# Local attention and a top-2 expert layer on one core: row tiles, a constant copy and weight splits on other turns, list products a turn behind GpSimd

## The chip, the cores and the metric

One core of a Trainium2 chip runs the whole program. The metric is the device time of one execution in microseconds; a kernel's number is the median of its runs. The engines are named as the profile names them: PE is TensorE (PEld its weight loads), DVE is VectorE, ACT is ScalarE, POOL is GpSimd, and SP is SyncE, which issues most DMAs.

## The reference

The work is an attention within chunks of 64 positions, followed by a layer of eight experts of which each token uses two.

```python
scores = scale * np.matmul(q_c, k_c.transpose(0, 1, 2, 4, 3))      # chunks of 64
attn = np.exp(scores - scores.max(-1)); attn /= attn.sum(-1) + 1e-9
x = (attn @ v_c) as (4608 tokens, 512)
noisy_logits = x @ w_gate + np.log1p(np.exp(x @ w_noise)) * noise   # (4608, 8)
top2 and their softmax weights, per token
for e in range(8):                                                  # w1 512x1024, w2 1024x512
    out[mask] += weight * (np.maximum(x[mask] @ w1[e], 0.0) @ w2[e])
```

All data are float32. The large products are made of three products of rounded halves (`three`, L305): each operand is split into a high part `h` and a rest `l`, and the product of the two rests is left out.

## The kernel before, in words

**Turns.** The tokens are 36 tiles of 128. `attend(it)` (L677) is one turn of a software pipeline over the tiles: in turn `it` PE computes the scores of tile `it` (L410), the value products of tile `it - 2` (L437), the transposed probabilities of tile `it - 1` (L426) and the transposed rows of tile `it - 3` (L457). Every fourth turn adds a gate product (L464), the next turn its sum (L476). DVE takes the maximum (`mx`, L414) and the difference (`pr`, L419) of the new tile, and the reciprocal and scaling (`rc`, `xs`) of tile `it - 2`. ACT does the exponential and the copies out of PSUM. SP loads q, k and v four turns ahead and stores each finished tile to `xbuf` in DRAM.

**Routing.** The tiles form five groups of 8, 8, 4, 8 and 8 tiles (numbered 0 to 4 here, `LAST` is 4). When the gate values of a group are there, a Python generator `route(g)` (L481) issues the group's routing in small pieces, and `step_route(n)` takes n pieces. So the number of pieces per turn sets where each routing instruction stands in the queues of all engines. A turn takes 10 pieces up to turn 34 and 15 after that; in the layers of the first two blocks each hook takes 2. The pieces of a group, in order: ACT's four functions (L494 to L497), seven empty pieces, five gate steps on DVE (`gu`, `gsp`), the eight-wide maxima and their indices (`gm`, `gmi`), the one-hot rows (`goh`) and their sum `gohb` (L527), seven empty pieces ahead of the rank products on PE (L535, L537), the ranks back on DVE (`gr`, L546), and then `gpf` (L582), the place of every token in the lists.

**List rows and list products.** After that the group has one row for each tile (L595 to L614). A row is a pair of one-hot matrices `gohp` (one half by POOL, L598, the other by two ACT functions, L599 and L600) and a matrix `grhs` (from `geq` on DVE, L602; the product on POOL, L606, for the last group on DVE). `place` (L588) multiplies the two on PE into bank 7 of PSUM (L590). A row is multiplied after two more have been built; three buffers of each operand hold them. At a group's end DVE adds the bank to `acc` (L622, L624), and after groups 1, 3 and 4 the lists of one block of expert 0 are finished and its rows gathered.

**Blocks.** Each expert's rows come in three blocks. `x_tile(i, k)` (L279) turns one tile of 128 gathered rows of block i (for the first three blocks four PE transposes, L288) and splits it (`xh` by ACT, `xl` by DVE). `layer1` (L307) and `layer2` (L346) then run the products; layer 1 of block 0 starts right behind the last turns, whose rests (turns 37 to 40) are put between its products by `hook_tail`. Block 0's three tiles are turned at the end of turns 33, 34 and 35 into PSUM banks 6, 6 and 5. Block 1's three tiles are turned within layer 2 of block 0, after the seventh of eight product triples of each row tile (hook `hook2_r`, L777). In layer 2 of block 1, `pieces()` (L215) copies the identity into `spread` (`xv`) and multiplies it with the lists (L222, L224) to make the row numbers for all later gathers.

**Splits.** Expert 0's first weights come in eight half loads (turns 11 to 18) and are split by `w_split` (L130) in turns 18, 19, 21, 22, 24, 25, 27 and 28: high part on ACT (L137), rest on POOL (L138).

All engines have their own queue in program order, so an instruction that waits holds everything behind it on its engine.

Of the kernel before, what the change touches and what calls it, by code (L numbers as in the profile page):

```python
# [8 lines left out]
FT = mybir.dt.float32  # L9
# [10 lines left out]
P = 128  # L20
NTOK = 4608
NT = NTOK // P
# [38 lines left out]
def kernel(ctx, tc, qT, kT, vh, wgn, noise, w1, w2, out, caps=CAPS):  # L61
    nc = tc.nc
# [10 lines left out]
    ident = consts.tile([P, P], FT, name="ident")  # L73
# [27 lines left out]
    for c in sorted(set(caps[1:])):  # L101
        n = caps.index(c, 1)
# [14 lines left out]
    place = {}  # L117
# [38 lines left out]

    NPE = nb
    AHEAD = [(1, 7), (2, 2), (2, 4), (2, 7)]
    LATE = [(1, 0), (1, 4), (2, 0), (2, 4)]
    groups = [(0, 8), (8, 8), (16, 4), (20, 8), (28, 8)]  # L160
    LAST = len(groups) - 1
# [6 lines left out]
    NL = NJ * NE  # L168
# [44 lines left out]
    xv = []  # L213

    def pieces():  # L215

        spread = xv[0].tile([P, 4, 4, 32], FT, name="xv")
        nc.vector.tensor_copy(spread, ident.rearrange("p (t c) -> p t c", t=4)[:, :, None, :].to_broadcast([P, 4, 4, 32]))
        tf = lfl
        for t in range(4):  # L220
            p = PS[:, 7, t * NJ * NE:(t + 1) * NJ * NE]
            nc.tensor.matmul(p, spread[:, t].rearrange("p a c -> p (a c)"), tf.rearrange("p j e -> p (j e)"),  # L222
                             start=True, stop=True)
            nc.tensor.matmul(PS[:, 7, 4 * NJ * NE + t * NE:4 * NJ * NE + (t + 1) * NE],  # L224
                             spread[:, t].rearrange("p a c -> p (a c)"), lwt[:, NJ - 1, :], start=True, stop=True)
        nc.vector.tensor_copy(wrep.rearrange("p t e -> p (t e)"), PS[:, 7, 4 * NJ * NE:4 * (NJ + 1) * NE])
        nc.vector.tensor_scalar(piece.rearrange("p t j e -> p (t j e)"), PS[:, 7, 0:4 * NJ * NE],
                                4.0, part, op0=OP.mult, op1=OP.add)
# [248 lines left out]
        nc.scalar.activation(Z[q][:, 4 * g - t0:4 * g - t0 + 4].rearrange("p g a e -> p (g a e)"), PS[:, 6, 0:64], AF.Copy)  # L477

    IDLE = 7

    def route(g):  # L481

# [102 lines left out]
        lp = PS[:, 7, 0:2 * NL]  # L585
        built = []

        def place(r, ohp, rhs):  # L588
            for k in range(2):
                nc.tensor.matmul(lp, ohp[:, k], rhs[:, k].rearrange("p c n -> p (c n)"),  # L590
                                 start=(r == 0 and k == 0), stop=(r == G - 1 and k == 1))

        B = nc.gpsimd if g < LAST else V
        n2 = [P, 2, NL]
        for r in range(G):  # L595
            t = t0 + r
            ohp = gate.tile([P, 2, P], FT, name="gohp", bufs=3)
            nc.gpsimd.tensor_scalar(ohp[:, 0], row_p, pf[:, 0, 0, r:r + 1], None, op0=OP.is_equal)  # L598
            nc.scalar.activation(ohp[:, 1], row_p, AF.Abs, scale=-1.0, bias=pf[:, 0, 1, r:r + 1])  # L599
            nc.scalar.activation(ohp[:, 1], ohp[:, 1], AF.Relu, scale=-1.0, bias=1.0)  # L600
            eq = gate.tile(n2, FT, name="geq", bufs=3)
            V.tensor_tensor(eq, row_je.rearrange("p j e -> p (j e)")[:, None, :].to_broadcast(n2),  # L602
                            pf[:, 1, :, r:r + 1].to_broadcast(n2), OP.is_equal)
            yield
            rhs = gate.tile([P, 2, 2, NL], FT, name="grhs", bufs=3)
            B.tensor_tensor(rhs, eq[:, :, None, :].to_broadcast([P, 2, 2, NL]),  # L606
                            vals[:, :, t, :, None].to_broadcast([P, 2, 2, NL]), OP.mult)
            yield
            yield
            built.append((r, ohp, rhs))  # L610
            if len(built) > 2:
                yield
                place(*built.pop(0))
            yield  # L614
        while built:
            for _ in range(3):
                yield
            place(*built.pop(0))
        yield
# [11 lines left out]
        if g == LAST:  # L631
            for c in range(2):
                for js in (slice(0, NJ // 2), slice(NJ // 2, NJ)):
                    n = [P, js.stop - js.start, NE, NE]
                    by = gate.tile([P, 2, 2, NL], FT, name="grhs", bufs=3).rearrange("p a b n -> p (a b n)")
                    by = by[:, 0:n[1] * NE * NE].rearrange("p (j r e) -> p j r e", r=NE, e=NE)
                    V.tensor_tensor(by, a4[:, c, js][:, :, None, :].to_broadcast(n),
                                    perm[:, None].to_broadcast(n), OP.mult)
                    V.tensor_reduce(accp[:, c, js], by, AX.X, OP.add)
                    yield  # L640
            finish_lists(lid, lwt, lfl, accp)
# [2 lines left out]

    def step_route(n):
        for _ in range(n):
            while routing:
                try:
                    next(routing[0])
                    break  # L650
                except StopIteration:
                    routing.pop(0)
# [22 lines left out]
        nc.sync.dma_start(staged[0, which, c][:, h * 512:h * 512 + 512], src)  # L675

    def attend(it):  # L677
        STEPS = 2 if it < 35 else 3
        if it < NT:
            scores(it)  # L680
        if it + 4 < NT:
            load_q(it + 4)
            load_k(it + 4)
        if 0 <= it - 2 < NT:
            pv(it - 2)
        if it + 4 < NT:
            load_v(it + 4)
        if 0 <= it - 2 < NT:
            norm_a(it - 2)
        if 0 <= it - 1 < NT:  # L690
            p_trans(it - 1)
        if 0 <= it - 3 < NT:
            x_trans(it - 3)
        if it - 5 >= 0 and (it - 5) % 4 == 3:
            gate_sum((it - 5) // 4)
            if grp_of[it - 5] != grp_of.get(it - 4):
                routing.append(route(grp_of[it - 5]))
        if it - 4 >= 0 and (it - 4) % 4 == 3:
            gate_mm((it - 4) // 4)
        if it < NT:  # L700
            soft_sub(it, soft_max(it))
            soft_exp(it)
        if 0 <= it - 2 < NT:
            norm_b(it - 2)
            norm_c(it - 2)
            if 0 <= it - (NT - 3) < 3:
                x_tile(0, it - (NT - 3), at=(6, 6, 5)[it - (NT - 3)])
            step_route(5 * STEPS)
        if it in (18, 19, 21, 22, 24, 25, 27, 28):
            w_split(0, 1, *wq.pop(0), eng=nc.gpsimd)  # L710
        if 11 <= it < 19:
            half_load(1, it - 11)
        if NT - 8 <= it < NT:
            half_load(2, it - NT + 8)
        if it == 8:
            nc.sync.dma_start(xbuf[0:P, :], zero)
        if NT - 3 <= it < NT:
            zero_out(2)
# [30 lines left out]
    for i in range(NBL + 1):  # L749
# [27 lines left out]
        def hook2_r(k, f):  # L777
            hook2_f(k, f)
            step_route(2)
            if i == 0 and f == 6 and k < len(nxt):  # L780
                x_tile(1, k)
            if i == 1 and (k, f) in LATE:
                x_tile(2, LATE.index((k, f)))
            if i == 1 and (k, f) == (1, 5):
# [23 lines left out]
        elif i == 1:  # L808
# [3 lines left out]
            xy = pb.enter_context(tc.tile_pool(name="xy", bufs=2))  # L812
            HF[0] = pb.enter_context(tc.tile_pool(name="hf", bufs=1)).tile([P, NF, max(c % P for c in caps[1:])], FT, name="hf")
            xv.append(pb.enter_context(tc.tile_pool(name="xv", bufs=1)))
            layer2(1, hook2_r)
        elif i != 2 and i != 3:
            layer2(i - 1, hook2_f)
# [135 lines left out]
```

## Time and profile before

| what | value |
| --- | --- |
| median of 3 runs | 997.32 us (996.1 to 998.82) |
| the profiled execution, as timed | 996.2 us |
| its span, first to last instruction | 994.4 us |
| mean granted TensorE clock | 0.99 |
| PE busy | 955.1 us (96%) |
| DVE, ACT, POOL busy | 459.3, 307.9, 485.4 us |
| HBM traffic over the span | 121 GB/s |

The profile comes from one execution. Its times count from the first instruction. A row of a timeline has the start, the duration, the engine, the line, the operation and its tiles (out<-in); a bracket at its end has the time the engine was idle just before it, and who ended that. Rows of the chain have start, length, engine, tile and line; there and in the timelines a float32 matmul is recorded as two, so that "x4" of L590 is one list row with its two products. "issue" is a wait for which the profile shows nothing.

### The profile page before, as it was taken

Reading aid. Unit: us, or ns where it says so; the run is one execution under the profiler, and the core shown is the slowest. Engines: PE = TensorE matmul, PEld = TensorE weight load, DVE = VectorE, ACT = ScalarE, POOL = GpSimd, SP = SyncE. Lnnn points to the kernel's source line nnn. Section 1 sums busy time; section 2 is a strip of 40 time slices with the busy share of each in tenths; the row PEclk is TensorE's granted clock in tenths of the full one; section 3 lists DMA queues with packets and bytes.
Section 4 is the critical chain, followed back from the end, with each engine's and each line's share of the span. In section 5 each row is a group of like instructions: output and inputs, shape, how many; then the busy total and the mean of one; then the engine's idle time right before and its main releaser. Section 6 shows DMA issues by size and latency. Waiting matters only on the chain.

```text
span 994.4 us, 18553 instructions
## 1 busy us (share of the span) xinstructions
PE 955.1 (96%) x7353; PEld 855.4 (86%) x7353; DVE 459.3 (46%) x1001; ACT 307.9 (31%) x689; POOL 485.4 (49%) x619
## 2 busy tenths in 40 slices
PE   6898989999999999999999999999999999999994
PEld 5677769888799998998899899989998999899984
DVE  6678876543445442534253434343444344434311
ACT  4667764312232221322131223122322231223100
POOL 1043534426677776177617772677167616601111
PEclk9989999999999999999999999999999999999998
DMA  9998968332513452245214522552245223511212
GB/s 336 377 340 271 323 228 310 63 102 54 146 46 81 111 151 50 44 122 150 51 33 128 148 51 36 135 140 58 68 96 140 58 70 94 136 20 22 32 25 41
DMA packets 60362, 121.54 MB, mean 122 GB/s; under 512 B 9280, under 2 KB 10176, under 8 KB 60272
## 3 DMA queue, kind: packets, MB, share of 16 engines
q1 hardware_dynamic: 40112, 81.64, 23.2%
q0 software_dynamic: 20160, 38.69, 20.8%
q8 instruction: 58, 0.95, 0.4%
q14 instruction: 32, 0.26, 0.1%
HBM read 81.56 MB, written 38.73 MB: 121 GB/s over the span
## 4 chain that ended last, share of the span: by engine, by line
PE 84%; DVE 2%; ACT 1%; issue 0%; POOL 0%; DVEq 0%; ACTq 0%; POOLq 0%
PE PS L305 80%; PE PS L590 1%; PE PS L334 1%; PE PS L288 0%; DVE xl L296 0%; ACT xh L295 0%; PE PS L464 0%; DVE o L343 0%; POOL grhs L606 0%; DVE xs L449 0%; PE PS L222 0%; ACT xt L458 0%; PE PS L437 0%; ACT gohp L599 0%; DVE gmi L518 0%
## 5 line engine op out<-in xcount | busy, mean ns | idle before, releaser
L260 POOL DMA_INDIRECT xg<-xbuf,piece x257 | 265.9, 1035 | 72.6 <-issue 66.3
L305 PE MATMUL PS<-xh,w1h 128*128 128x384 f32 (+2 forms) x768 | 262.9, 342 | 1.9 <-ACT xh L295 1.1
L305 PE MATMUL PS<-xl,w1h 128*128 128x384 f32 (+2 forms) x768 | 260.5, 339 | 0.3 <-DVE xl L296 0.3
L305 PE MATMUL PS<-xh,w1l 128*128 128x384 f32 (+2 forms) x768 | 260.6, 339 | 0.0
L272 POOL DMA_INDIRECT out<-o,lid x73 | 116.9, 1601 | 246.5 <-DVE o L343 234.4
L305 PE MATMUL PS<-w2h,hh 128*128 128x512 f32 x584 | 229.5, 393 | 0.0
L305 PE MATMUL PS<-w2h,hl 128*128 128x512 f32 x584 | 228.4, 391 | 0.0
L305 PE MATMUL PS<-w2l,hh 128*128 128x512 f32 x584 | 228.3, 391 | 0.0
L323 ACT ACTIVATE hh<-PS 128x384 fp32r<-128x384 f32 (+1 forms) x192 | 93.9, 490 | 362.3 <-PE PS L305 362.3
L324 DVE SCALAR_TENSOR_TENSOR hl<-PS,hh 128x384 fp32r<-128x384 f32 (+1 forms) x192 | 107.0, 558 | 181.1 <-ACT hh L323 181.1
L343 DVE TENSOR_SCALAR o<-PS,lwt 128x512 f32<-128x512 f32 x73 | 54.7, 749 | 235.4 <-PE PS L305 235.4
L305 PEld LDWEIGHTS PS<-xh,w1h 128*128 128x128 f32 x768 | 144.3, 188 | 5.4 <-ACT xh L295 1.5
L305 PEld LDWEIGHTS PS<-xl,w1h 128*128 128x128 f32 x768 | 144.3, 188 | 2.3 <-DVE xl L296 0.5
L305 PEld LDWEIGHTS PS<-xh,w1l 128*128 128x128 f32 x768 | 144.2, 188 | 0.9
L305 PEld LDWEIGHTS PS<-w2h,hl 128*128 128x128 f32 x584 | 109.5, 188 | 23.6
L305 PEld LDWEIGHTS PS<-w2h,hh 128*128 128x128 f32 x584 | 109.7, 188 | 23.2 <-issue 0.8
L305 PEld LDWEIGHTS PS<-w2l,hh 128*128 128x128 f32 x584 | 109.7, 188 | 22.4
L295 ACT ACTIVATE xh<-y 128x512 fp32r<-128x512 f32 x67 | 41.2, 615 | 104.8 <-DVE y L292 104.8
L598 POOL TENSOR_SCALAR gohp<-row_p,gpf 128x128 f32<-128x128 f32 x36 | 25.1, 707 | 95.8 <-DVE gpf L582 71.6
L296 DVE TENSOR_TENSOR xl<-y,xh 128x512 fp32r<-128x512 f32 x67 | 45.0, 672 | 48.0 <-ACT xh L295 48.0
L292 DVE STREAM_TRANSPOSE y<-xg 128x512 f32<-128x512 f32 x67 | 45.6, 680 | 3.2 <-DMA xg<-xbuf,piece 3.2
L138 DVE TENSOR_TENSOR w2l<-st,w2h 128x512 fp32r<-128x512 f32 x64 | 44.4, 693 | 0.0
(139 smaller groups left out, 783.7 us busy)
## 6 DMA issues: line engine op xcount, KB each, us to landing
st<-in_w SPq DMA_DIRECT2D x56, 512.0 KB, 5.0
out<-zero SPq DMA_DIRECT2D x37, 256.0 KB, 4.0
vb<-in_vh SPq DMA_DIRECT2D x36, 260.0 KB, 4.9
qp<-in_qT SPq DMA_DIRECT2D x36, 256.0 KB, 4.5
kb<-in_kT SPq DMA_DIRECT2D x36, 256.0 KB, 5.3
xbuf<-xs SPq DMA_DIRECT2D x36, 256.0 KB, 4.4
xg<-xbuf,piece POOLq DMA_INDIRECT x257, 2.7
st<-in_w SPq DMA_DIRECT2D x16, 256.0 KB, 5.7
```

The lines of the kernel that those rows point to most:

```text
L138: (eng or nc.vector).tensor_sub(lo[:, s], st[:, s], hi[:, s].bitcast(FT))
L260: nc.gpsimd.indirect_dma_start(out=XG[e, j][:, t * P:(t + 1) * P], out_offset=None, in_=xpieces, in_offset=bass.IndirectOffsetOnAxis(ap=pi ...
L272: s = nc.gpsimd.indirect_dma_start(out=to, out_offset=bass.IndirectOffsetOnAxis(ap=rows, axis=0), in_=o, in_offset=None, compute_op=OP.add)
L292: nc.vector.transpose(y[:, 0:4 * r], x[:, 0:4 * r])
L295: nc.scalar.activation(oh, src, AF.Copy)
L296: nc.vector.tensor_sub(ol, src, oh.bitcast(FT))
L305: nc.tensor.matmul(p, a, b, start=first and n == 0, stop=last and n == 2)
L323: nc.scalar.activation(hh[:, 0:m], p, AF.Relu)
L324: nc.vector.scalar_tensor_tensor(hl[:, 0:m], p, 0.0, hh[:, 0:m].bitcast(FT), op0=OP.max, op1=OP.subtract)
L334: nc.tensor.matmul(p[32 * q:32 * q + 32, 0:P], HF[0][:, f, 32 * t:32 * t + 32], w[:, q * P:(q + 1) * P], start=(f == 0), stop=(f == NF - 1))
L343: nc.vector.tensor_scalar(o[0:r], p[0:r], weights_of(i, j)[0:r], None, op0=OP.mult)
L598: nc.gpsimd.tensor_scalar(ohp[:, 0], row_p, pf[:, 0, 0, r:r + 1], None, op0=OP.is_equal)
```

## The change

It does five things; none changes what is computed.

1. A turn takes 11 pieces of routing instead of 10 up to turn 34, 15 after that as before.
2. A list row is multiplied when it is `LAG` pieces old (9 up to turn 35, 6 after that) or when more than two wait, at the start of the next row; the rows' operands get four buffers each.
3. Block 0's third tile is turned at the start of turn 36 into bank 0, not at the end of turn 35 into bank 5. Block 1's three tiles are turned after triple 6 of row tile 0 and triples 2 and 6 of row tile 1 (counted from 0).
4. The splits stand in turns 21 to 25 and 30 to 32, the half loads in turns 13 to 20.
5. `spread` is copied ahead of layer 2 of block 1, not within `pieces()`.

```diff
+    SECOND = [(0, 6), (1, 2), (1, 6)]
...
     def pieces():
-        spread = xv[0].tile([P, 4, 4, 32], FT, name="xv")
-        nc.vector.tensor_copy(spread, ident.rearrange(...).to_broadcast([P, 4, 4, 32]))
+        spread = xv[1]
...
+    clock, LAG = [0], [9]
...
         for r in range(G):
+            while built and (clock[0] - built[0][3] >= LAG[0] or len(built) > 2):
+                place(*built.pop(0))
             t = t0 + r
-            ohp = gate.tile([P, 2, P], FT, name="gohp", bufs=3)
+            ohp = gate.tile([P, 2, P], FT, name="gohp", bufs=4)
...
             yield
             yield
-            built.append((r, ohp, rhs))
-            if len(built) > 2:
-                yield
-                place(*built.pop(0))
+            yield
+            built.append((r, ohp, rhs, clock[0]))
             yield
         while built:
-            for _ in range(3):
+            while clock[0] - built[0][3] < LAG[0]:
                 yield
             place(*built.pop(0))
...
     def step_route(n):
         for _ in range(n):
+            clock[0] += 1
...
     def attend(it):
-        STEPS = 2 if it < 35 else 3
+        LAG[0] = 9 if it < NT else 6
         if it < NT:
             scores(it)
+        if it == NT:
+            x_tile(0, 2, at=0)
...
-            if 0 <= it - (NT - 3) < 3:
-                x_tile(0, it - (NT - 3), at=(6, 6, 5)[it - (NT - 3)])
-            step_route(5 * STEPS)
-        if it in (18, 19, 21, 22, 24, 25, 27, 28):
+            if 0 <= it - (NT - 3) < 2:
+                x_tile(0, it - (NT - 3), at=6)
+            step_route(11 if it < 35 else 15)
+        if it in (21, 22, 23, 24, 25, 30, 31, 32):
             w_split(0, 1, *wq.pop(0), eng=nc.gpsimd)
-        if 11 <= it < 19:
-            half_load(1, it - 11)
+        if 13 <= it < 21:
+            half_load(1, it - 13)
...
-            if i == 0 and f == 6 and k < len(nxt):
-                x_tile(1, k)
+            if i == 0 and (k, f) in SECOND:
+                x_tile(1, SECOND.index((k, f)))
...
             xv.append(pb.enter_context(tc.tile_pool(name="xv", bufs=1)))
+            xv.append(xv[0].tile([P, 4, 4, 32], FT, name="xv"))
+            nc.vector.tensor_copy(xv[1], ident.rearrange(...).to_broadcast([P, 4, 4, 32]))
             layer2(1, hook2_r)
```

Three places show how the queues change. The first is PE's queue in turns 14 and 15, before: scores (L410), value products, the two transposes, and in turn 15 the gate product and the rank products of group 0.

```order
L410 MATMUL PS<-kb,qp 64x64 x16
L437 MATMUL PS<-vb,pts 64x65 x16
L426 MATMUL PS<-ident,pr 128x128 x4
L457 MATMUL PS<-ident,xs 128x128 x4
L410 MATMUL PS<-kb,qp 64x64 x16
L437 MATMUL PS<-vb,pts 64x65 x16
L426 MATMUL PS<-ident,pr 128x128 x4
L457 MATMUL PS<-ident,xs 128x128 x4
L464 MATMUL PS<-xt,wg 32x512 x4
L535 LDWEIGHTS before
L535 MATMUL PS<-gohb,before 128x72
```

The same queue of the changed kernel, from the scores of turn 14 on:

```order
L410 MATMUL PS<-kb,qp 64x64 x16
L437 MATMUL PS<-vb,pts 64x65 x16
L426 MATMUL PS<-ident,pr 128x128 x4
L457 MATMUL PS<-ident,xs 128x128 x4
L536 LDWEIGHTS before
L536 MATMUL PS<-gohb,before 128x72
L538 LDWEIGHTS ones
L538 MATMUL PS<-gohb,ones 128x64
```

The rank products now stand ahead of the scores of turn 15, in the turn in which DVE makes `gohb`. The same holds for group 2 in turn 30 and group 3 in turn 36.

The second place is PE's queue behind the last tile's value products (L437), where layer 1 of block 0 (L305) has begun. Before, group 3's first list product comes 33 matmuls of layer 1 behind them; these are the rows just ahead of it:

```order
L305 MATMUL PS<-xh_136,w1l_2170 128x384
L476 MATMUL PS<-sel,ls 128x16 x4
L305 MATMUL PS<-xh_136,w1h_1426 128x384
L305 MATMUL PS<-xl_137,w1h_1426 128x384
L305 MATMUL PS<-xh_136,w1l_1427 128x384
L590 MATMUL PS<-grhs,gohp 128x160 x2
```

In the changed kernel the whole stretch from the value products to that first list product (now L591) is this:

```order
L437 MATMUL PS<-vb,pts 64x65 x16
L457 MATMUL PS<-ident,xs 128x128 x4
L305 MATMUL PS<-xh_136,w1h_2014 128x384
L305 MATMUL PS<-xl_137,w1h_2014 128x384
L305 MATMUL PS<-xh_136,w1l_2015 128x384
L591 MATMUL PS<-grhs,gohp 128x160 x2
L305 MATMUL PS<-xh_136,w1h_2507 128x384
```

Only one transpose and three matmuls of layer 1 are left between them.

The third place is DVE's queue at the end of layer 2 of block 0: `gpf` and the list rows (`geq`, `grhs`) of group 4, the third row tile of block 1 (`xl`), and the weighing of a finished row tile (`o`). Before:

```order
L576 TENSOR_TENSOR vals<-gex,vals 128x8
L580 TENSOR_SCALAR gpj<-lii 128x16
L581 TENSOR_TENSOR gpj<-lii,gpj 128x16
L582 CAST gpf<-gpj 128x32
L602 TENSOR_TENSOR geq<-row_je,gpf 128x160
L606 TENSOR_TENSOR grhs<-geq,vals 128x320
L602 TENSOR_TENSOR geq<-row_je,gpf 128x160
L296 TENSOR_TENSOR xl_3251<-PS,xh_3250 128x4x128
L606 TENSOR_TENSOR grhs<-geq,vals 128x320
```

And in the changed kernel:

```order
L577 TENSOR_TENSOR vals<-gex,vals 128x8
L296 TENSOR_TENSOR xl_3268<-PS,xh_3267 128x4x128
L581 TENSOR_SCALAR gpj<-lii 128x16
L582 TENSOR_TENSOR gpj<-lii,gpj 128x16
L583 CAST gpf<-gpj 128x32
L605 TENSOR_TENSOR geq<-row_je,gpf 128x160
L343 TENSOR_SCALAR o<-PS,lwt_126 128x512
L609 TENSOR_TENSOR grhs<-geq,vals 128x320
```

The row tile's `xl` has moved from behind two list rows to ahead of the first.

More of the change, by code (lines that the diff above doesn't have):

```diff
@@ L215, in pieces @@
     def pieces():
-        spread = xv[0].tile([P, 4, 4, 32], FT, name="xv")
-        nc.vector.tensor_copy(spread, ident.rearrange("p (t c) -> p t c", t=4)[:, :, None, :].to_broadcast([P, 4, 4, 32]))
+        spread = xv[1]
         tf = lfl
@@ L586, in route, with place @@
         built = []
-        def place(r, ohp, rhs):
+        def place(r, ohp, rhs, at):
             for k in range(2):
@@ L604, in route @@
             yield
-            rhs = gate.tile([P, 2, 2, NL], FT, name="grhs", bufs=3)
+            rhs = gate.tile([P, 2, 2, NL], FT, name="grhs", bufs=4)
             B.tensor_tensor(rhs, eq[:, :, None, :].to_broadcast([P, 2, 2, NL]),
@@ L634, in route @@
                     n = [P, js.stop - js.start, NE, NE]
-                    by = gate.tile([P, 2, 2, NL], FT, name="grhs", bufs=3).rearrange("p a b n -> p (a b n)")
+                    by = gate.tile([P, 2, 2, NL], FT, name="grhs", bufs=4).rearrange("p a b n -> p (a b n)")
                     by = by[:, 0:n[1] * NE * NE].rearrange("p (j r e) -> p j r e", r=NE, e=NE)
@@ L814 @@
             xv.append(pb.enter_context(tc.tile_pool(name="xv", bufs=1)))
+            xv.append(xv[0].tile([P, 4, 4, 32], FT, name="xv"))
+            nc.vector.tensor_copy(xv[1], ident.rearrange("p (t c) -> p t c", t=4)[:, :, None, :].to_broadcast([P, 4, 4, 32]))
             layer2(1, hook2_r)
```

## The prediction

> **What bounds the kernel now.** I read the busy times by stage first, then the vector engine's waits in the first of those stages, then the timeline at each place the diff touches. Columns of the first view: stretch, its length, busy time of PE, PEld, DVE, ACT and POOL with counts, granted clock, DMA share, GB/s.
>
> ```profile
> span 994.4 us, 18553 instructions
> ```
> ```profile
> 41.00:132.00 91.00, 78.28 (x1893) 65.43 (x1886) 74.13 (x242) 67.37 (x171) 38.19 (x48) 0.96 0.92 314
> 132.00:150.00 18.00, 15.89 (x194) 12.57 (x187) 13.09 (x62) 11.20 (x30) 5.23 (x8) 1.00 0.60 219
> 150.00:184.00 34.00, 34.00 (x197) 30.82 (x196) 19.39 (x83) 12.31 (x32) 14.47 (x19) 1.00 0.70 231
> 184.00:232.00 48.00, 45.51 (x243) 40.60 (x242) 22.61 (x54) 11.52 (x29) 18.83 (x25) 0.96 0.35 87
> 232.00:994.00 762.00, 749.95 (x4033) 680.39 (x4032) 303.65 (x503) 184.64 (x387) 405.93 (x508) 0.99 0.35 82
> ```
>
> From 232 us on TensorE is the bound, and the diff moves nothing there. From 150 to 184 it is busy all the time. So everything is decided in three stretches: the attention turns from 41 to 132 (turn 12 to the end of turn 34), the hand-over to expert 0 from 132 to 150, and the two holes that leave PE idle for 48.00 - 45.51 = 2.5 us between 184 and 232. In the attention turns PE idles 12.7 us and DVE 16.9 us, and neither carries the stage alone. The waits of DVE there (us in total, times, longest):
>
> ```profile
> DVE mx L414 <- PE PS L410: 5.4, 7, 1.3
> DVE gu L501 <- ACT gsp L497: 2.3, 1, 2.3
> DVE xl L296 <- ACT xh L295: 1.6, 2, 0.9
> DVE gr L546 <- PE PS L537: 1.6, 1, 1.6
> DVE acc L622 <- PE PS L590: 1.5, 1, 1.5
> ```
>
> The reader is to see that a turn is a ring: PE's scores, DVE's max and subtraction, then the next scores. The next row shows the scores of turn 15 going out only after the subtraction of turn 14. What DVE has to wait for inside a turn therefore lengthens it.
>
> ```profile
> 52.92 1.13 PE L410 MATMUL PS<-kb,qp 64*64 64x64 f32 x32 [0.64 <-DVE pr L419]
> ```
>
> **Part by part. Eleven steps a turn, and the rank products.** Rank products (one "before", eight "ones") that stood a turn behind the one-hot sum `gohb` now stand at the end of the same turn in turns 14 and 30, and likewise in turn 36. Now DVE goes from `gohb` to the next max without a pause, and the rank products take 57.83 to 58.22, 0.4 us:
>
> ```profile
> 54.06 0.23 DVE L527 TENSOR_TENSOR gohb<-goh 128x64 bf16<-128x64 f32 x1
> 54.20 0.17 DVE L529 TENSOR_TENSOR gex<-gm 128x8 f32<-128x8 f32 x1
> 54.28 0.69 DVE L414 TENSOR_REDUCE mx<-PS 128x8 f32<-128x512 f32 x1
> ```
> ```profile
> 57.83 0.21 PE L535 MATMUL PS<-gohb,before 128*128 128x72 bf16 x1
> 57.87 0.35 PE L537 MATMUL PS<-gohb,ones 128*128 128x64 bf16 x8
> ```
>
> Afterwards, PE's queue holds next turn's scores behind products that wait for `gohb`; DVE then waits 0.4 for the products and about 0.7 for the scores (as long as a max row, 0.69): 1.1 us in each of two turns, +2.2. In return `gr` finds its products done, -1.6. Group 1's first gate step `gu` moves into turn 20, right behind ACT's four-function chain, as group 0's does in turn 12, where it waited 2.3 us: bounds 0 and +2.3, I take +0.8, since PE's gate sum delays the next turn less there. `acc` of group 0 waits for one product pair less, -0.3.
>
> **Products a turn behind POOL.** Group 2's first product held PE:
>
> ```profile
> 129.22 0.81 PE L590 MATMUL PS<-grhs,gohp 128*128 128x160 f32 x4 [0.95 <-POOL grhs L606]
> ```
>
> Its rows are now built in turns 32 and 33 and multiplied in 33 and 34, so this 0.95 goes; a fourth buffer of each operand removes POOL's wait for PE. Taken -1.0. Three rows in turns 25 and 32 put six ACT half-operations in a row instead of four, behind a split; that may cost up to 1 us a turn, which I put into the range.
>
> **The splits.** Eight splits leave turns 18 to 28 for 21 to 25 and 30 to 32, mostly turns without list rows. What one does to DVE when it meets a gate step with two SBUF inputs:
>
> ```profile
> 81.93 0.22 DVE L507 TENSOR_TENSOR gsp<-gsp,nz 128x64 f32<-128x64 f32 x1
> 82.19 1.32 DVE L509 TENSOR_TENSOR gsp<-gsp,gz 128x64 f32<-128x64 f32 x1
> ```
> ```profile
> 82.16 1.27 POOL L138 TENSOR_TENSOR w1l<-st,w1h 128x512 fp32r<-128x512 f32 x1 [5.15 <-ACT w1h L137]
> ```
>
> The same kind of step took 0.22 us alone and 1.32 beside the split: 1.1 us lost. The Trainium skill, page "SBUF — State Buffer", section "Who interferes with whom", states it as a rule: a DVE instruction with two SBUF inputs and a GpSimd instruction that reads SBUF exclude each other for a whole instruction. The trace agrees, with 1.32 against 0.22; the rule speaks against this change, which moves splits to the turns where such gate steps stand. I take 0: a split starts about when the gate's short steps end (82.16 above, behind four of them), list rows lose their neighbour in turns 27 and 28, and in turn 30 DVE waits anyway. Bounds: -2.2 (two such losses gone) to +3.3 (three new ones).
>
> Sum of the attention turns: +2.2 - 1.6 + 0.8 - 0.3 - 1.0 + 0 = +0.1, called 0, with -3 to +4 around it. The half loads two turns later change no wait: no row above names a load.
>
> **The hand-over.** `V` is the value product of the last tile:
>
> ```profile
> 140.41 0.70 PE L437 MATMUL PS<-vb,pts 64*64 64x65 f32 x32
> ...
> 142.25 0.19 PE L535 MATMUL PS<-gohb,before 128*128 128x72 bf16 x1 [0.55 <-DVE gohb L527]
> ...
> 147.17 0.45 PE L305 MATMUL PS<-xh,w1h 128*128 128x384 f32 x1 [0.83 <-DVE hl L324]
> ```
> ```profile
> 142.52 0.16 ACT rc L442
> ```
> ```profile
> 145.42 0.66 POOL L598 TENSOR_SCALAR gohp<-row_p,gpf 128x128 f32<-128x128 f32 x1 [11.35 <-PE PS L457]
> 146.05 0.72 POOL L606 TENSOR_TENSOR grhs<-geq,vals 128x320 f32<-128x320 f32 x1
> ```
> ```profile
> 132.99 0.43 PE PS L457 x4
> ```
> ```profile
> 153.73 0.54 PE PS L590 x4
> 154.27 1.56 PE PS L305 x9
> ```
>
> Now PE loses 0.55 + 0.83 there, and stands at expert 0's third output block 147.17 - 141.11 = 6.1 us after `V`. In the changed queue group 3's first list product follows `V` after one transpose (0.43) and three matmuls (1.56 / 3 = 0.52). It needs everything from `rc` to the first `grhs`: 142.52 to 146.77, 4.25 us. PE idles 4.25 - 0.95 = 3.3. The third block then starts 4.25 + 0.54 + 1.56 + 0.43 + 0.52 + 0.54 + 0.52 = 8.4 after `V`, with two products (1.08) already done, and `hl` is long ready: 8.4 - 6.1 - 1.1 = +1.2. The rank products ahead of `V` instead of behind it, waiting for `gohb` of their own turn, add 0.3. Together +1.5; bounds 0 (DVE reaches `gpf` earlier than I reckon, since most of the gate now lies in turn 35) and +3.3. The third row tile, moved to turn 36 and bank 0, is covered by these waits; uncovered it is 0.4 of PE.
>
> **The second block's rows.** Its third tile is turned eight matmul triples earlier, and its `xl` stands ahead of group 4's list rows on DVE, so the wait ahead of layer 1 goes: -1.07 - 0.28 = -1.35.
>
> ```profile
> 185.58 0.44 PE L305 MATMUL PS<-xh,w1h 128*128 128x384 f32 x1 [1.07 <-ACT xh L295]
> 186.31 0.44 PE L305 MATMUL PS<-xl,w1h 128*128 128x384 f32 x1 [0.28 <-DVE xl L296]
> ```
>
> What is late next is the first product of group 4, now inside layer 2; by the same DVE rows it is ready about when PE comes. At worst it gives the 1.35 back.
>
> **The constant copy.** It is made before layer 2 of the second block, under matmuls, so this wait goes, -1.14:
>
> ```profile
> 219.05 0.42 PE L222 MATMUL PS<-lfl,xv 128*128 128x80 f32 x2 [1.14 <-DVE xv L218]
> ```
>
> Sum: 0 + 1.5 - 1.35 - 1.14 = -1.0. The profiled execution took 996.2 us (994.4 and 1.8 around it), 1.1 below the median 997.32 of the runs, so the median of the changed kernel should be 996.3.
>
> **The rivals.** Faster: the granted clock. Behind the copy's hole it fell to half:
>
> ```profile
> 220.00:224.00 4.00, 4.00 (x16) 3.42 (x16) 0.68 (x3) 0.00 (x0) 1.11 (x2) 0.58 0.00 0
> ```
> ```profile
> 221.17 3.56 PE PS L305 x9
> 224.73 0.44 PE PS L288 x4
> 225.17 2.75 PE PS L305 x12
> ```
>
> Nine matmuls took 0.40 each instead of 0.23, 1.5 us. If the hole made the clock fall, it goes with the hole; with the gate's waits also falling out well (attention at -2), the sum is -1.0 - 1.5 - 2 = -4.5: 992.8. For it: one drop follows the hole at once. Against it: the 1.35 us idle ahead of 186 us had none (0.96 over 48 us is about one drop of 3.4 us). Chance 0.3. The Trainium skill, page "TensorE: Matmul & The Clock Gate", section "What's actually happening", says the clock is halved after an idle window of about 3.4 us in a free-running raster; the 1.14 us hole followed by eight tiny products is no idle window of that length, so by the rule the drop's cause is open.
>
> Slower: PE's queue stalls in order. The rank products and the first list product stand too close behind what DVE must finish; at the upper bounds the hand-over costs 3.3 and the turns 4, against -2.5: +4.8, 1002.1. It decides from 5.5 us of new waits on. Chance 0.15.
>
> Slower by the splits: if each of the five in gate turns (21, 22, 23, 30, 31) meets a two-input step, 5 x 1.1 = 5.5 us are added: 1001.8. For it stands the one loss shown; against it, the splits that now stand beside list rows lose such a partner. Chance 0.07. This is what the Trainium skill's page "SBUF — State Buffer" would make of the move.
>
> The change could also do nothing where it means to: if DVE's ring alone sets the turns, all moves there are free and only +1.5 - 2.5 is left; that lies inside my forecast.
>
> **How the numbers follow.** A measurement here can tell 0.3%, 3.0 us. Forecast: no such difference, chance 0.48; its own range is 994.3 to 1000.3. The range of 8 in 10 reaches to the faster rival's number and half way into the slower one: 992.6 to 1001. Faster 0.30, same 0.48, slower 0.22.
>
> **What would show it.** Right: no PE wait for `xv` and none for `xl` ahead of the second block's layer 1; a PE wait of about 3 us at the first list product some 1 us behind the last `V`; about 1 us of DVE waiting for scores behind `gohb` in turns 14 and 30; the stretch from turn 12 to turn 34 at 88 to 95 us. Wrong: that first product does not wait, gate steps of 1.3 us appear beside several splits, or the clock drops at other places than now.

## The result and the profile after

The changed kernel takes 1003.55 us (median of 6 runs, 1002.27 to 1007.01) against 996.53 for the kernel before in the same comparison: a ratio of 1.0077, with a 95% interval of 1.0062 to 1.0092. It is 7 us slower. The forecast, 996.3 and "no difference that can be told", is wrong, and 1003.55 lies outside the range that ended at 1001.0. The profiled execution of after is 8.0 us longer than that of before.

First the page's busy row of PE and its neighbours, of after and then of before.

```profile
span 1002.4 us, 18535 instructions
...
PE 959.2 (96%) x7353; PEld 859.4 (86%) x7353; DVE 458.3 (46%) x1001; ACT 307.7 (31%) x689; POOL 483.5 (48%) x619
```
```profile
PE 955.1 (96%) x7353; PEld 855.4 (86%) x7353; DVE 459.3 (46%) x1001; ACT 307.9 (31%) x689; POOL 485.4 (49%) x619
```

The same 7353 matmuls keep PE busy 4.1 us longer, and PE is idle 1002.4 - 959.2 = 43.2 us instead of 994.4 - 955.1 = 39.3, 3.9 us more. So half of the loss is waiting and half is slower matmuls. Next, busy time by stage, in the columns that the prediction named; the stages are cut at the max of turn 12, the max of turn 35 and the 300th expert matmul of each kernel. After, then before:

```profile
42.70:139.10 96.40, 81.45 (x1888) 68.69 (x1881) 74.21 (x244) 67.96 (x175) 39.65 (x51) 0.93 0.85 291
139.10:227.40 88.30, 82.87 (x522) 73.56 (x521) 50.16 (x190) 32.27 (x82) 29.79 (x40) 0.94 0.53 174
227.40:1002.40 775.00, 763.02 (x4105) 691.18 (x4103) 307.54 (x510) 186.20 (x390) 411.29 (x515) 1.00 0.36 82
```
```profile
41.40:132.10 90.70, 77.98 (x1871) 65.13 (x1865) 74.23 (x242) 67.07 (x171) 38.23 (x49) 0.96 0.92 314
132.10:215.90 83.80, 80.34 (x552) 71.66 (x543) 50.70 (x190) 33.35 (x86) 32.43 (x43) 1.00 0.56 181
215.90:994.40 778.50, 764.91 (x4105) 692.63 (x4103) 307.95 (x511) 186.22 (x390) 412.00 (x515) 0.99 0.35 81
```

The attention turns grew by 5.7 us and the hand-over with the first 300 expert matmuls by 4.5; the rest shrank by 3.5, and 1.3 us lie ahead of turn 12, where the change moves nothing (a later pair of traces has -0.3 there). The clock column shows where the slower matmuls are: 0.96 became 0.93, and 1.00 became 0.94.

What PE waits for between turn 12 and 160 us (waited for; us in total, times, longest), after and then before:

```profile
PE PS L536 <- DVE gohb L528: 6.7, 3, 2.8
PE PS L410 <- DVE pr L419: 6.4, 4, 3.0
PE PS L591 <- POOL grhs L609: 3.5, 3, 2.6
```
```profile
PE PS L410 <- DVE pr L419: 6.9, 7, 2.0
PE PS L590 <- POOL grhs L606: 1.9, 3, 0.9
```

Waits of the rank products for `gohb` are new as a leading row: three, 6.7 us. Here they are on PE's timeline (start, us, idle before and its releaser), with the first list product of group 3:

```profile
55.44 0.19 PE L536 MATMUL PS<-gohb,before 128*128 128x72 bf16 x1 [1.80 <-DVE gohb L528]
...
120.84 0.18 PE L536 MATMUL PS<-gohb,before 128*128 128x40 bf16 x1 [2.81 <-DVE gohb L528]
...
146.49 0.22 PE L536 MATMUL PS<-gohb,before 128*128 128x72 bf16 x1 [2.07 <-DVE gohb L528]
...
151.66 0.52 PE L305 MATMUL PS<-xh,w1l 128*128 128x384 f32 x1
154.80 0.81 PE L591 MATMUL PS<-grhs,gohp 128*128 128x160 f32 x4 [2.62 <-POOL grhs L609]
```
```profile
214.29 0.33 PE L305 MATMUL PS<-xh,w1l 128*128 128x384 f32 x1
```

These are turns 14, 30 and 36 and the hand-over: 1.80, 2.81, 2.07 and 2.62 us. The matmul at 151.66 took 0.52 us and the same form at 214.29 took 0.33. The hand-over of after, cut at the raster in which its clock changes:

```profile
138.50:141.90 3.40, 3.32 (x69) 2.04 (x63) 3.21 (x9) 2.43 (x8) 0.00 (x0) 1.00 0.94 295
141.90:145.40 3.50, 2.15 (x35) 1.94 (x26) 3.31 (x26) 2.52 (x7) 0.00 (x0) 0.99 0.73 256
145.40:148.80 3.40, 2.31 (x15) 2.10 (x14) 1.06 (x10) 0.21 (x1) 0.00 (x0) 0.50 0.39 145
148.80:152.20 3.40, 3.38 (x40) 2.52 (x39) 1.57 (x8) 0.86 (x2) 0.00 (x0) 0.50 0.00 0
152.20:155.60 3.40, 0.80 (x5) 0.80 (x6) 1.62 (x8) 1.92 (x6) 2.35 (x4) 1.00 0.95 360
155.60:159.00 3.40, 3.40 (x15) 3.30 (x13) 1.45 (x3) 1.01 (x2) 2.71 (x5) 0.50 0.90 329
159.00:162.40 3.40, 3.40 (x24) 2.31 (x23) 1.06 (x2) 2.23 (x6) 0.85 (x2) 1.00 1.00 381
```

Read PE's busy time of a row against the clock of the next. The window from 152.2 holds the wait for the first list product, PE is busy 0.80 of 3.40 us, and the next window runs at 0.50. The wait in turn 36 leaves 2.15 of 3.50 and then 2.31 of 3.40, and two windows run at 0.50. Between turn 12 and 240 us the trace of after has seven such half-clock windows, that of before three. One of the three that before had is gone: the one behind the wait for `xv`.

### The profile page after: what moved, and what is told of

It reads as the page before. It is cut to its first block, busy times and chain, and to the rows that moved or that the text cites. A ratio compares the mean times of both kernels' runs of the same rounds, so it can differ in the third digit from the quotient of the medians.

```text
span 1002.4 us, 18535 instructions
## 1 busy us (share of the span) xinstructions
PE 959.2 (96%) x7353; PEld 859.4 (86%) x7353; DVE 458.3 (46%) x1001; ACT 307.7 (31%) x689; POOL 483.5 (48%) x619
## 4 chain that ended last, share of the span: by engine, by line
PE 83%; DVE 2%; issue 0%; POOL 0%; ACT 0%; DVEq 0%
PE PS L305 80%; PE PS L334 1%; PE PS L591 1%; PE PS L288 0%; DVE gaccp L640 0%; DVE grhs L638 0%; DVE xs L449 0%; PE PS L437 0%; PE PS L222 0%; PE PS L464 0%; DVE hl L324 0%; DVE gmi L519 0%; PE PS L457 0%; PE PS L476 0%; DVE o L343 0%
## 5 line engine op out<-in xcount | busy, mean ns | idle before, releaser
L305 PE MATMUL PS<-xh,w1h 128*128 128x384 f32 (+2 forms) x768 | 263.7, 343 | 0.3 <-DVE hl L324 0.3
L305 PE MATMUL PS<-xh,w1l 128*128 128x384 f32 (+2 forms) x768 | 261.4, 340 | 0.0
L305 PE MATMUL PS<-xl,w1h 128*128 128x384 f32 (+2 forms) x768 | 261.2, 340 | 0.0
L305 PE MATMUL PS<-w2h,hh 128*128 128x512 f32 x584 | 228.7, 392 | 0.0
L305 PE MATMUL PS<-w2h,hl 128*128 128x512 f32 x584 | 227.7, 390 | 0.0
L305 PE MATMUL PS<-w2l,hh 128*128 128x512 f32 x584 | 227.6, 390 | 0.0
L305 PEld LDWEIGHTS PS<-xh,w1h 128*128 128x128 f32 x768 | 145.0, 189 | 3.7 <-DVE hl L324 0.9
L305 PEld LDWEIGHTS PS<-xl,w1h 128*128 128x128 f32 x768 | 144.9, 189 | 1.8
L305 PEld LDWEIGHTS PS<-xh,w1l 128*128 128x128 f32 x768 | 145.0, 189 | 1.0
L305 PEld LDWEIGHTS PS<-w2h,hl 128*128 128x128 f32 x584 | 109.2, 187 | 23.5
L305 PEld LDWEIGHTS PS<-w2h,hh 128*128 128x128 f32 x584 | 109.2, 187 | 23.0 <-issue 0.8
L305 PEld LDWEIGHTS PS<-w2l,hh 128*128 128x128 f32 x584 | 109.2, 187 | 22.5
```

The costliest lines, as they stand in the source:

```text
L305: nc.tensor.matmul(p, a, b, start=first and n == 0, stop=last and n == 2)
```

## The experiments

Two theories were set against each other. The **stall theory**: TensorE's queue stalls where a product now stands too close behind its producer, and the idle window halves the clock for what follows. The **split theory**, from the prediction's rivals: the moved GpSimd splits hold up VectorE's gate steps. Chips differ: the kernel before takes 997 us on some and 1004 on others, so the runs are compared by their ratio to the kernel before on the same chip, and 0.001 is 1 us.

**The changed kernel again.** On a chip where before takes 1004.02, and later on one where it takes 996.97:

> The changed kernel once more, beside the kernel before on the same chip as the three kernels below. All theories: a ratio of 1.006 to 1.009, as measured first.

> The changed kernel beside the two above on the same chip, for the comparison. All theories: a ratio to before of 1.004 to 1.008.

Ratios 1.0046 (1.0032 to 1.0061), below what was expected, and 1.0071 (1.0056 to 1.0086), within it. The sign is sure; the size may depend on the chip.

**The splits, from both sides.** Into the kernel before they are put alone; out of the changed kernel they are taken:

```
-        if it in (18, 19, 21, 22, 24, 25, 27, 28):
+        if it in (21, 22, 23, 24, 25, 30, 31, 32):
...
-        if 11 <= it < 19:
-            half_load(1, it - 11)
+        if 13 <= it < 21:
+            half_load(1, it - 13)
```

> The kernel before with one part of the change alone: the eight splits in turns 21 to 25 and 30 to 32 and the half loads from turn 13. Split theory: the loss comes from here, 3 to 7 us slower than before (ratio 1.003 to 1.007). Stall theory: no TensorE wait hangs on them, ratio 0.998 to 1.002.

> The changed kernel with the eight splits and the eight half loads in the turns that they had before (18, 19, 21, 22, 24, 25, 27, 28; loads from turn 11). Split theory: the loss sits in the moved splits, so most of it goes, 997 to 999.5 us, and the 1.3-us gate step in turn 21 is 0.2 us long. Stall theory: the rank waits in turns 14, 30 and 36 and the wait at the first list product stay, 1002.5 to 1004.5.

The first gave 1.000 (0.9982 to 1.0017): put into the kernel before, the moved splits cost nothing that can be measured, and the split theory falls. The second gave 1.003 (1.001 to 1.0051), still slower, with its three rank waits in place (5.3 us). That is less than the changed kernel's 1.0046 to 1.0077, but the changed kernel was not run on that chip. In the trace, turns 12 to 34 take 95.2 us, within the 94.7 to 98.4 of the three traces of the changed kernel; a small part for the splits is not excluded.

**Row tiles and constant copy alone**, in the kernel before:

```
+    SECOND = [(0, 6), (1, 2), (1, 6)]
...
-        spread = xv[0].tile([P, 4, 4, 32], FT, name="xv")
...
+        spread = xv[1]
...
-            if i == 0 and f == 6 and k < len(nxt):
-                x_tile(1, k)
+            if i == 0 and (k, f) in SECOND:
+                x_tile(1, SECOND.index((k, f)))
...
+            xv.append(xv[0].tile([P, 4, 4, 32], FT, name="xv"))
...
```

> The kernel before with two parts of the change alone: the constant copy ahead of the second block, and the second block's row tiles at (0,6), (1,2) and (1,6). If these parts gain what the idle rows say: 996.5 - 1.35 (waits for xh and xl) - 1.14 (wait for xv) = 994.0, and 1.7 less, 992.3, if the half-clock window at 220.6 us goes with the wait ahead of it; range 991.5 to 994.5. If their waits only move elsewhere: 995.5 to 997.

0.9960 (0.9941 to 0.9979), 4 us faster: both waits and the half-clock window are gone. In the four traces that have the copy in its old place, this window stands right behind the wait for `xv`; in none of the others does it.

**Rank products later**, in the changed kernel:

```
-        for _ in range(IDLE + 4 if g == LAST else IDLE):
+        for _ in range(IDLE + 4):
```

> The changed kernel with four more idle steps ahead of every rank product, so that none stands in the turn of its own gohb. Stall theory (TensorE waits for gohb at the head of its queue in turns 14, 30 and 36, 1.80, 2.81 and 2.07 us in the trace of after, and the granted clock halves in the window behind each): the three waits shrink to under 0.7 us each and the half-clock windows behind turns 14 and 30 go; 995 to 999.5 us against 1003.6 for the changed kernel. Split theory (the moved splits hold up VectorE through the shared memory port): nothing of this is touched, 1002.5 to 1004.5.

0.9966 (0.9946 to 0.9986), by the ratios 8 to 11 us better than the changed kernel. PE's waits in its trace:

```profile
PE PS L410 <- DVE pr L419: 8.3, 5, 2.3
PE PS L591 <- POOL grhs L609: 1.9, 2, 1.5
PE PS L536 <- DVE gohb L528: 1.9, 1, 1.9
```

The time is at least as good as the stall theory expected (995 to 999.5 us beside 996.53 for before, ratios of 0.998 to 1.003), the place is not. In turn 14 a wait of 1.81 us for `pr` takes the place of the rank wait, turn 36 still waits 1.9, and half-clock windows still stand behind turns 14 and 30. What went entirely is the wait at group 3's first list product, and two of three half-clock windows of the hand-over.

**The rank products alone**, queued right behind `gohb` in the kernel before:

```
-        for _ in range(IDLE + 4 if g == LAST else IDLE):
+        for _ in range(IDLE + 4 if g == LAST else 0):
```

with `2 * IDLE` steps behind them.

> The kernel before with one thing of the change alone: the rank products of groups 0 to 3 queued directly behind their gohb, in the same turn (14, 22, 31 and 36), and the idle steps taken from there put behind them, so that every VectorE, ScalarE and GpSimd step keeps its turn. Stall theory: three to four waits of 1.5 to 2.8 us ahead of the rank products, with a half-clock window behind most of them: 5 to 11 us slower than before. Split theory: rank products next to their gohb cost nothing, within 1.5 us of before.

1.0025 (1.001 to 1.004): the right sign, but 2.5 us where 5 to 11 were expected. Two waits of 5.4 us together appear (turn 14 and the hand-over), not four, and the one in turn 14 covers a wait for `pr` that was 1.65 us long in a later trace of before.

**One rank wait alone**, group 2's of turn 30, out of the changed kernel (`IDLE + 4` for groups 2 and LAST):

> The changed kernel with the four more idle steps for group 2 alone, so that its rank products leave turn 30; group 3, which follows it in the same list of steps, moves four steps along in the tail. Stall theory: the wait of 2.81 us in turn 30 (118.03 to 120.84 us in the trace of after) falls under 0.7 us and the half-clock windows around it go, while the wait in turn 14 stays: 3 to 5 us less than the changed kernel, a ratio to before of 1.000 to 1.003. Split theory: unchanged, 1.004 to 1.008.

1.0063 (1.0039 to 1.0086), no gain, a miss. Its rank wait in turn 30 is gone, but on this chip V waits in pieces there, behind something that the profile only calls issue:

```profile
117.77 0.47 PE L437 MATMUL PS<-vb,pts 64*64 64x65 f32 x17 [0.24 <-issue]
118.53 0.35 PE L437 MATMUL PS<-vb,pts 64*64 64x65 f32 x3 [0.28 <-issue]
119.26 0.31 PE L437 MATMUL PS<-vb,pts 64*64 64x65 f32 x3 [0.39 <-issue]
120.00 0.58 PE L437 MATMUL PS<-vb,pts 64*64 64x65 f32 x9 [0.43 <-issue]
```

The unchanged changed kernel has the same rows on such a chip, and its rank products then wait only this long:

```profile
122.99 0.19 PE L536 MATMUL PS<-gohb,before 128*128 128x40 bf16 x1 [0.33 <-DVE gohb L528]
```

So 2.81 us of the first trace were 0.33 there: on such a chip there was next to nothing to take away.

**The first list product later**, in the changed kernel:

```
-        LAG[0] = 9 if it < NT else 6
+        LAG[0] = 9 if it < NT else 20
```

> The changed kernel with group 3's list products held back 20 steps instead of 6, so that the first stands nine 384-column matmuls (some 3 us) later in TensorE's queue. Stall theory: the wait of 2.62 us at the first list product falls to under 0.5 us and the half-clock window behind it goes: 2.5 to 4.5 us less than the changed kernel, a ratio to before of 1.003 to 1.006. Split theory: the wait was hidden by what comes later, ratio 1.007 to 1.009.

1.0012 (0.9994 to 1.003), 3.4 us better than the changed kernel on the same chip. The wait at the first list product, 3.52 us in the changed kernel's trace on that chip, is gone, and from turn 35 to the 100th expert matmul the trace has 35.45 us instead of 39.81; a row tile waits 1.86 us for its gather instead.

**All of them later, and the list that is then late.**

```
-        for _ in range(IDLE + 4 if g == LAST else IDLE):
+        for _ in range(IDLE + 8 if g == 3 else IDLE + 4):
...
-        LAG[0] = 9 if it < NT else 6
+        LAG[0] = 11 if it < NT else 9
```

> The changed kernel with the rank products four steps later (eight for group 3) and the list products held back 11 and 9 steps instead of 9 and 6, so that none of them stands at the head of TensorE's queue ahead of its data. Stall theory: no wait of over 1 us on gohb or grhs is left, and the row tiles and the constant copy keep their gain of some 4 us: a ratio to before of 0.990 to 0.996. Split theory: the moved splits are still there, so the ratio stays over 1.000.

1.0038 (1.0022 to 1.0054), a miss. A wait of 2.59 us for `grhs` is left in turn 34. Group 3's lists release the gathers of the second block, whose first row tile stands at a fixed place in PE's queue:

```profile
178.59 1.12 PE L288 MATMUL PS<-ident,xg 128*128 128x128 f32 x4 [4.37 <-DMA xg<-xbuf,lid]
```

With `SECOND = [(1, 2), (1, 6), (2, 2)]` on top:

> The mended kernel with its three row tiles of the second block two to four steps later, at (1,2), (1,6) and (2,2), behind the landing of their gathers. If mended lost its gain to the 4.37-us wait for xg and the two half-clock windows behind it (174.22 to 184.1 us in its trace): that wait goes, 4.4 to 7.8 us less than mended, a ratio to before of 0.996 to 0.9995. If something else held mended up: within 0.002 of its 1.0038.

0.999 (0.997 to 1.001): the wait falls to 2.0 us and 4.8 us come back. Here the delay in a queue was paid for at the next reader.

**Idle time or clock.** Unread matmuls in the waits, which then keep their length:

```
+    def fill(n):
+        for _ in range(n):
+            nc.tensor.matmul(PS[:, 7, 384:512], before, ones, start=True, stop=True)
...
+        fill(FILL.get(g, 0))
         nc.tensor.matmul(rk, before, ohb, start=True, stop=False)
...
+            if (g, r) == (3, 0):
+                fill(36)
```

> The changed kernel with matmuls that nobody reads put into TensorE's queue ahead of the rank products of turns 14 (24), 30 (40) and 36 (28) and ahead of group 3's first list product (36): the waits stay, TensorE is busy in them. If an idle window is what halves the clock: the half-clock windows that stand behind these waits in the trace of after (56.6, 121.5, 145.4 and 155.6 us) go, and the time falls by 3 to 6 us to 998 to 1000.5 although work was added. If the idle time alone costs, and the half-clock windows come for another reason: they stay, 1003.5 to 1006.

1.0028 (1.0009 to 1.0047), in part as expected. No half-clock window is left in the hand-over, but in turn 30 the 40 unread matmuls themselves met half clock, took 4.22 us and made the turn 7.3 us long instead of 3.8. So the filling was tried in the hand-over alone (`FILL = {3: 28}`), together with a kernel mended there alone:

> The changed kernel with unread matmuls in TensorE's queue ahead of group 3's rank products (28) and of its first list product (36) alone; every wait stays. If idle windows halve the clock and that is half of the hand-over's loss: no half-clock window between turn 35 and the 100th expert matmul, 2 to 4 us less than the changed kernel. If the idle time alone costs: the same time as the changed kernel within 1 us.

1.0035 (1.0022 to 1.0048) against 1.0071 for the changed kernel beside it: 3.6 us less, for added work. The two traces place 2.0 us of it in the hand-over (37.34 against 39.38 us from turn 35 to the 100th expert matmul), where the changed kernel has two half-clock windows and the filled one none; 1.9 us lie ahead of turn 12, where nothing was filled. First the changed kernel on that chip, on its raster:

```profile
142.90:146.30 3.40, 1.52 (x19) 1.27 (x18) 1.75 (x11) 0.26 (x2) 0.00 (x0) 1.00 0.51 193
146.30:149.70 3.40, 3.10 (x40) 2.48 (x39) 1.86 (x10) 0.86 (x2) 0.00 (x0) 0.50 0.03 12
149.70:153.10 3.40, 1.09 (x7) 1.09 (x8) 1.34 (x6) 1.91 (x6) 2.64 (x4) 1.00 1.00 380
153.10:156.50 3.40, 3.40 (x14) 3.30 (x13) 1.64 (x3) 1.28 (x3) 2.77 (x6) 0.50 0.89 328
```

Then the filled one:

```profile
141.10:144.50 3.40, 2.90 (x61) 2.52 (x61) 1.49 (x10) 0.21 (x1) 0.00 (x0) 1.00 0.41 154
144.50:147.90 3.40, 2.50 (x47) 2.20 (x40) 2.49 (x13) 1.05 (x3) 0.04 (x1) 1.00 0.29 105
147.90:151.30 3.40, 2.95 (x31) 2.78 (x29) 0.70 (x3) 2.25 (x8) 3.40 (x6) 1.00 1.01 383
151.30:154.70 3.40, 3.40 (x24) 2.83 (x26) 1.97 (x4) 2.55 (x6) 3.00 (x4) 1.00 1.00 379
```

1.52 and 1.09 us of busy time are each followed by clock 0.50; filled to 2.50 and 2.95, no window is.

**The hand-over mended alone:**

```
+        for _ in range(IDLE + 8 if g == 3 else IDLE + 4 if g == LAST else IDLE):
...
+        LAG[0] = 9
...
+    SECOND = [(1, 2), (1, 6), (2, 2)]
```

> The changed kernel mended in the hand-over alone: group 3's rank products eight steps later, list products held back nine steps there too, the second block's row tiles at (1,2), (1,6) and (2,2); the attention turns stay as in the changed kernel. If most of the loss sits in the hand-over (the stretch from turn 35 to the 300th expert matmul is 88.28 us in the trace of after, 83.81 in before): that stretch falls to 82.5 to 84.5 us and the ratio to before is 0.999 to 1.003. If most of it sits in turns 12 to 34: within 2 us of the changed kernel.

0.9988 (0.9973 to 1.0003), 8.3 us less than the changed kernel on the same chip and a little less than expected. The kernel before was traced there too:

> The kernel before, for its trace on this chip: whether the half-clock windows behind turns 20 to 22 and 29 to 30 and the V products of turn 29 that wait behind issue, which every kernel on the later chips shows, are its own too. If so, the span is some 5 us over the 994.4 us of the first trace, and turns 12 to 34 take 92 to 94 us instead of 90.7.

998.25 us, a span of 996.5, and no V row of turn 29 that waits in pieces: it ran on a chip without that trait, and why some chips show it stays open. Of the half-clock windows asked about it has the one behind turn 21 (86.4 us), which is thus not the change's own.

Three traces of one chip can now be set side by side. Turns 12 to 34 and the hand-over (up to the 100th expert matmul) of before, the changed kernel and the one mended in the hand-over, in this order:

```profile
42.94:133.95 91.01, 77.83 (x1871) 65.02 (x1868) 74.32 (x242) 66.64 (x171) 38.26 (x49) 0.96 0.92 313
133.95:168.97 35.02, 32.93 (x293) 29.43 (x285) 21.58 (x84) 21.35 (x57) 13.21 (x20) 1.00 0.81 300
```
```profile
42.62:137.34 94.72, 78.77 (x1886) 66.17 (x1881) 73.59 (x244) 68.11 (x175) 39.65 (x51) 0.96 0.87 296
137.34:176.72 39.38, 34.25 (x265) 30.47 (x264) 22.59 (x93) 20.47 (x53) 13.84 (x19) 0.91 0.77 280
```
```profile
43.30:139.45 96.15, 80.00 (x1886) 66.84 (x1881) 72.93 (x243) 68.01 (x175) 39.72 (x51) 0.95 0.86 291
139.45:172.10 32.65, 31.48 (x264) 27.87 (x263) 21.69 (x83) 20.12 (x53) 11.48 (x17) 1.00 0.89 328
```

The change makes the hand-over 4.4 us longer, with the clock at 0.91 instead of 1.00; the mended one is 6.7 us shorter than the changed one, and so 2.4 shorter than that of before. The 8.3 us that mending gave back are therefore more than the hand-over of the change had cost. Up to the 600th expert matmul the three need 154.17, 154.62 and 146.95 us from turn 35 on, since the row tiles and the copy gain there. The third row tile keeps its new place in the mended kernel, so it is not what made the hand-over longer.

**A version that beats both**: the kernel with row tiles and copy, four list buffers, and group 2's list products behind all its rows.

```
-            if len(built) > 2:
+            if len(built) > 2 and g != 2:
...
-            for _ in range(3):
+            for _ in range(2 if g == 2 else 3):
```

> The kernel before with the constant copy and the row tiles of the change, four list buffers, and group 2's list products placed behind all four of its rows instead of two at a time. Stall theory: the 1.67-us wait for grhs in turn 34 that the kernel with copy and rows shows (129.90 to 131.56 us) and the half-clock window behind it go, on top of the 4 us of copy and rows: a ratio to before of 0.992 to 0.996. If that wait was hidden by later work: 0.995 to 0.998.

0.9947 (0.993 to 0.9964): 5 us faster than before, 10 to 13 faster than the changed kernel. No wait for `grhs` of over 0.6 us is left in its attention turns, but one of 1.58 us for `pr` stands in the place of the last, and the half-clock window behind it, which was expected to go, stays (132.0 us). The gain over row tiles and copy alone, 0.0013, is within the two intervals.

## Why the prediction was wrong, by its steps

Cut by stages, the traces show what each part cost. This is the kernel after less the kernel before, for the first pair and for the pair of the later chip (after_beside and before_beside):

| part | predicted, us | first pair, us | later pair, us |
|---|---|---|---|
| up to turn 12 | 0 | +1.3 | -0.3 |
| attention turns, 12 to 34, with the splits | 0 | +5.7 | +3.7 |
| hand-over, turn 35 to the 100th expert matmul | +1.5 | +5.4 | +4.4 |
| row tiles and constant copy, to the 600th | -2.5 | -3.9 | -3.9 |
| the rest | 0 | -0.5 | -0.5 |
| the whole span | -1.0 | +8.0 | +3.3 |

Each column is a pair of single executions; by the medians the later pair lies 7.2 us apart. The row tiles and the copy agree with their own run (0.9960). Two list rows, 1.1 us of PE's work, stand in the turns of after and in the hand-over of before, so for equal work the turns cost some 1.1 us less than the table says and the hand-over as much more. Two steps of the prediction failed.

- **The hand-over, put at +1.5 with a bound of 3.3.** The prediction's 3.3 us of idleness at the first list product was right in kind and nearly in size (2.62). The rank products ahead of `V` were put at 0.3 and waited 2.07, because VectorE has the fifteen steps of turn 35 ahead of `gohb` (the gate up to its sixth index search, 141.28 to 144.03), then the `xl` of the third row tile, which the change moved there (0.67), `xs` (0.69) and the gate's rest, while TensorE was through with its transposes and the gate sum at 144.42. And both were priced at their own length only: half-clock windows follow them, three in the trace of after and two in the later one, where filling the waits took 2.0 us off. Moving both products later, in hand_only, took the whole loss away.
- **The attention turns, put at 0**, are the other step. On one chip they take 98.4 us in the changed kernel (after_again) and 96.8 in late_first, whose turns are the same, but 91.95 in mended, which keeps the eleven steps and queues the rank and list products later. At most 1.6 us of that are three list rows that mended leaves to the hand-over. So the place of these products is most of what the turns lost, too. How the loss is shared among turns 14, 21 and 30 no run separates, and the eleven steps were never taken back alone.
- **The rank products in turns 14 and 30.** The prediction read the price off VectorE's ring, 1.1 us a turn. VectorE did wait 1.04 us for the scores, twice:

```profile
56.51 0.69 DVE L414 TENSOR_REDUCE mx<-PS 128x8 f32<-128x512 f32 x1 [1.04 <-PE PS L410]
...
121.90 0.69 DVE L414 TENSOR_REDUCE mx<-PS 128x8 f32<-128x512 f32 x1 [1.04 <-PE PS L410]
```

  But TensorE waited 1.80 and 2.81 for `gohb`, and a half-clock window followed each. Turn 14 grew from 2.81 to 3.57 us; turn 30 did not grow, and turn 31, most of it at half clock, went from 2.71 to 4.54.
- **Turn 21**, which the prediction left out. Eleven steps instead of ten put all eight maxima and six of eight index searches into one turn, and the scores waited 2.98 us instead of 2.03, again with half clock behind them; the later trace of before has that window too, behind 2.04.
- **`gu`, `gr`, `acc`**: `gu` waited 3.3 us in two turns instead of 2.3 in one, so +0.8 was close; `gr` waited 0.9 instead of 1.6, not 0 as the -1.6 had it, and `acc` moved by under 1 us.
- **Products a turn behind POOL**: group 2's waits of 0.95 and 0.47 are gone in the trace of after, as the -1.0 said, but two of 0.46 stand at group 1's products.
- **The splits**: one gate step of 1.30 us beside a split in turn 21, as one of 1.32 before. The exclusion that the Trainium skill's "SBUF — State Buffer", section "Who interferes with whom", states shows again; but the whole move gave 1.000 in the kernel before, so the +5.5 that the rival made of it did not come.
- **The row tiles and the copy**: the waits went as priced, -1.35 and -1.14. The first piece product of after starts without one:

```profile
229.17 0.34 PE L222 MATMUL PS<-lfl,xv 128*128 128x80 f32 x2
```

  The clock drop behind the copy went with it, as the faster rival had it (1.5 us).
- **The rivals.** The slower one, PE's queue stalling in order, is what happened. Its 1002.1 was near in part by luck, as it held no price for the clock; its chance of 0.15 was too low, since the forecast itself had named all four of its waits. The faster rival's mechanism was at work too. That the clock reacts to idle windows was weighed only where the change took a hole away, and not for the holes that it makes: with the rank waits priced too low, this is the error behind the size.
- **The signs.** Those named for "right" came, but for the turns, which left their 88 to 95 us with 96.4 in the first trace. Of those named for "wrong", the clock dropped at other places than before.

## What to carry to other kernels

In a queue that runs in order, a product that is moved earlier must be checked against its producer's position in the other engine's queue, and one moved later against its next reader: mended lost 4.8 us to a row tile that it had left in place. As an estimate from these traces, price a TensorE hole of 2 us or more at its length plus 1 to 1.7 us for the window behind it (filling took 2.0 us off over two windows; 1.7 is half the length of one), and ask of every new hole what was asked of every one removed. Where a change bundles parts, the sum can hide a gain: here, by the ratios, 4 us of it lay under 11 us of loss.

## What the runs showed of the clock

Over the 18 profiled executions, cut into windows of 3.41 us on each trace's own raster between 18 and 980 us, a full-clock window in which PE was busy for less than 40% was followed by a half-clock window in 32 of 32 cases, one with 40 to 80% in 39 of 213, and one with 80% or more in none of 4705. Once halved, the clock stayed so for another window in 9 of 9 cases when PE was busy for less than 80%, and in 1 of 68 when it was busy for 90% or more.

The Trainium skill's page "TensorE: Matmul & The Clock Gate", section "What's actually happening", names an idle window of about 3.4 us in a free-running raster as what halves the clock. Raster and length agree with these traces: in each, the half-clock windows start whole multiples of 3.41 us apart. The window need not be idle, though: 1.52 of 3.40 us busy was enough, and the prediction, which read the rule as asking for 3.4 us of idleness, was wrong to call the drop's cause open by it. Between 40 and 80% busy the share alone doesn't decide; what else does is open.
